# Moving a block of TensorE's program: even quads' P.V behind the loop's end, quad 1's keys directly behind quad 0's

## The chip, the cores and the metric

The kernel runs on one core of a Trainium2 chip. The metric is the device time of one execution in microseconds (us). Before the change it is 192.4 us, the median of three runs (191.73 to 192.55).

## What is computed

One decode step: attention of a single query over a cache of 4096 positions, 32 heads of 128, mixed by a gate with a small MLP. Cut from the reference:

```python
q = (x @ wq).reshape(B, Sq, Hq, Dh)                 # x: 1 x 512, 32 heads of 128
scores = einsum("bhqd,bhkd->bhqk", q, k) * (Dh ** -0.5)
p = softmax(scores)                                  # over 4096 positions
o = einsum("bhqk,bhkd->bhqd", p, v)
a = o.reshape(B, Sq, Hq * Dh) @ wo
h = relu(x @ w1 + b1); b = (h * h) @ w2 + b2
g = sigmoid((x * gate_w).sum(-1))
out = g * a + (1 - g) * b
```

Everything is bf16. Keys and values together are 67 MB of the 78 MB that are read; each is used once.

## The kernel before

**Tiling.** The 32 heads are handled as eight quads of four heads. A quad's keys are one tile of 128 partitions (32 per head) by 128 blocks of 128 numbers, loaded by one DMA of 4 MB; its values likewise. The four slots of `KV` hold two key tiles and two value tiles, so a quad's keys take the slot of the quad two before.

**A quad's work.** Of 128 key blocks, VectorE takes 48: a multiply and a sum over each of four parts of 12 blocks (`ttr`, L679 and L683). TensorE takes the other 80, in ten groups of eight: it transposes a group (`transposes`, L456), ScalarE copies the result to SBUF (`evac`, L351), and TensorE multiplies it with the query (`scores`, L463). `keys(a, behind)` issues the ten groups with the scores two groups behind the transposes; `a` is the parity of the quad. Then ScalarE copies the scores together (L357), VectorE takes the maximum per partition into `mp` (`smax`, L688), TensorE turns it into a row (`max_rows`, L484), VectorE reduces it (`gmax`, L692), TensorE spreads it again (`max_cols`, L488), ScalarE takes the exponentials (L368), and TensorE forms the denominators and P.V (`pv`, L493 and L497).

**The order of loads.** SyncE issues all large loads through one queue in a fixed order: wq, K0, K1, V0, w1, K2, wo's first quarter, K3, V1, K4, V2, K5, V3 and so on. A key tile is issued when its slot's last quad has been through VectorE's four parts (`s_sd`) and TensorE's ten groups of transposes (`s_t`); a value tile from V2 on when the P.V two before is done; wo's first quarter when the last of the query's eight projections is done (`s_qps`), which sits in `keys(1)` of the first turn. A load that waits holds all loads behind it.

**TensorE's program.** It is a loop written by hand with basic blocks, a register `turn_no`, branches and jumps; a turn handles an even and an odd quad. The blocks stand in the program in the order in which the code opens them: loop, h1, m1, m2, out, rows, first, k0, c1, v0, k1, r0, next, mlp, end. A branch whose target stands next falls through to it. In turn 0 the way is loop, first, k0 (`keys(0)`), r0 (`max_rows(0)`, `keys(1)`, `max_cols(0)`), next. From turn 1 on c1 (`max_cols(1)`) and v0 (`pv(0)`) come between k0 and r0; from turn 2 on also out and rows, blocks further up that are jumped to and come back by a jump to v0 and k1. Turn 4 runs only the odd quad's rest and the last even quad's P.V, with the MLP's first half (`mlp`) in between; turn 5 runs the last P.V and goes to `end`. In turn 0, then, k0 branches to r0 past c1, v0 and k1, 273 instructions; from turn 1 on c1 follows k0 in line and r0 follows k1 in line.

TensorE's whole program is 1748 instructions. `keys(1)`, with what stands between r0 and next, is 370 of them.

Of the kernel before, what the change touches and what calls it, by code (L numbers as in the profile page):

```python
# [5 lines left out]
def bass_gated_mix__gqa_block_cached__dense_activation_squared_relu__decode_kernel(  # L6
# [17 lines left out]
    ALU = mybir.AluOpType  # L24
# [55 lines left out]
    with ctx:  # L80
# [323 lines left out]
        def _(eng):  # L404
# [5 lines left out]
            turn_no = eng.alloc_register("turn_no")  # L410
# [3 lines left out]
            def at(name):  # L414
                stretch.close()
                if name == "end":
                    nc.switch_bb("pe_end")
                else:
                    stretch.enter_context(nc.body(f"pe_{name}", valid_engines=[mybir.EngineType.PE]))

            def go(name):
                eng.br(f"pe_{name}")

            def branch(op, n, then, other):
                eng.br_cmp(turn_no, n, f"pe_{then}", f"pe_{other}", op)

            def part(name):

                go(name)
                at(name)  # L430

            def only(name, op, n):

                branch(op, n, name, name + "_in")
                at(name + "_in")
# [14 lines left out]
            def take(sm, n=1):  # L450
                eng.wait_ge(sm, n).then_inc(sm, -n)  # L451

            def transposes(a, g):
                for y in range(GB):
                    b = Y_BLOCKS[GB * g + y]
                    mm = eng.transpose(KP[(GQ * a + g) % NKP][:, y * 128:(y + 1) * 128], key(a, b), ident[:, :])  # L456
                mm.then_inc(s_t, 1)

            def scores(a, g):
                take(s_ev)  # L460
                for y in range(GB):
                    c = GB * g + y
                    mm = eng.matmul(pS[:, R * c:R * c + R], kT[:, (GQ * a + g) % NT, y * 128:(y + 1) * 128],  # L463
                                    qc2[:, a, :], start=True, stop=True)
                mm.then_inc(s_s2, 1)

            def keys(a, behind):
                take(s_kp)
                for g in range(GQ):
                    transposes(a, g)  # L470
                    if g >= 2:
                        if g == 2:
                            take(s_q2)
                        scores(a, g - 2)
                    if g in behind:
                        only(f"q{a}{g}", "IS_GE", 1)
                        behind[g]()
                        part(f"q{a}{g}")
                scores(a, GQ - 2)
                scores(a, GQ - 1)  # L480

            def max_rows(a):
                take(s_mp)
                eng.transpose(MT, mp[:, a:a + 1], identf[:, :]).then_inc(s_mt, 1)  # L484

            def max_cols(a):
                take(s_dg)
                eng.matmul(MB[:, a:a + 1], dg[:, a, :], onesf[0:1, 0:1],  # L488
                           start=True, stop=True).then_inc(s_mb, 1)
# [62 lines left out]
            extra = [{}, {8: zero}]  # L552
# [52 lines left out]

            part("k0")
            keys(0, extra[0])
            branch("IS_LT", 1, "r0", "c1")
            at("c1")
            max_cols(1)  # L610
            branch("IS_GE", 2, "out", "v0")
# [2 lines left out]
            branch("IS_GE", 2, "rows", "k1")  # L614
            at("k1")
            eng.wait_ge(s_e, 1)
            part("r0")
            max_rows(0)
            keys(1, extra[1])
            max_cols(0)  # L620
            part("next")
            eng.reg_alu(turn_no, turn_no, 1, op=ALU.add)
            go("loop")

            at("mlp")
            mlp_h()
# [157 lines left out]
```

## Time and profile before

| | |
|---|---|
| time, median of 3 runs | 192.4 us (191.73 to 192.55) |
| profiled execution, its own time | 192.3 us |
| its span, first to last instruction | 190.8 us |
| mean granted TensorE clock | 0.727 |
| TensorE busy (matmul) | 136.8 us, 72% |
| VectorE busy | 122.5 us, 64% |
| ScalarE busy | 115.6 us, 61% |
| read from HBM | 78.32 MB, 410 GB/s over the span |
| queue q1 (all loads) | 4296 packets, 96.7% of 16 engines' span |
| queue q8 (kind: instruction) | 7 packets, 0.11 MB |

How to read it: the profile is one execution, and times within it count from the span's start. The engines are PE (TensorE's matmuls), PEld (its weight loads), DVE (VectorE), ACT (ScalarE), POOL (GpSimd) and SP (SyncE, which only issues loads here; SPq in the timeline). A timeline row gives start, duration, engine, line, operation, output and inputs, how many were merged, and in brackets how long the engine had been idle and what ended that. "PEq L451" is TensorE's own sequencer, at the semaphore step of the helper `take`; it stands there whatever the semaphore waited for. The DMA lines are shares of the core's 16 DMA engines and rates in equal slices. Each load also leaves 16 semaphore increments in the trace, one from each DMA engine; the last of them is the landing that the kernel waits for. Packets have a queue, a start, a duration and a size.

### The profile page before, as it was taken

Reading aid. Unit: us, or ns where it says so; the run is one execution under the profiler, and the core shown is the slowest. Engines: PE = TensorE matmul, PEld = TensorE weight load, DVE = VectorE, ACT = ScalarE, POOL = GpSimd, SP = SyncE. Lnnn points to the kernel's source line nnn. Section 1 sums busy time; section 2 is a strip of 40 time slices with the busy share of each in tenths; the row PEclk is TensorE's granted clock in tenths of the full one; section 3 lists DMA queues with packets and bytes.
Section 4 is the critical chain, followed back from the end, with each engine's and each line's share of the span. In section 5 each row is a group of like instructions: output and inputs, shape, how many; then the busy total and the mean of one; then the engine's idle time right before and its main releaser. Section 6 shows DMA issues by size and latency. Waiting matters only on the chain. (4 is left out here: it accounts for less than half of the span.)

```text
span 190.8 us, 6235 instructions
## 1 busy us (share of the span) xinstructions
PE 136.8 (72%) x2688; PEld 119.8 (63%) x2688; DVE 122.5 (64%) x123; ACT 115.6 (61%) x242; POOL 6.0 (3%) x13
## 2 busy tenths in 40 slices
PE   0009397607874979988995999769786596899855
PEld 0003176405763968977984997659575595789844
DVE  1100099989924999999999399829990699701011
ACT  3004669813998998798597569829961398450000
POOL 4000000000250000000000000000000000000000
PEclk9999969955897596695588559657955579555555
DMA  6999999989989999999999999999999999989991
GB/s 217 441 440 440 440 436 433 440 378 467 434 338 380 433 433 433 434 433 440 433 440 434 433 433 440 426 419 440 397 448 433 440 433 433 434 374 421 421 388 45
DMA packets 4321, 78.47 MB, mean 411 GB/s; under 512 B 499, under 2 KB 853, under 8 KB 1110
## 3 DMA queue, kind: packets, MB, share of 16 engines
q1 hardware_dynamic: 4296, 78.32, 96.7%
q8 instruction: 7, 0.11, 0.2%
q14 instruction: 4, 0.03, 0.0%
q10 hardware_dynamic: 14, 0.01, 0.0%
HBM read 78.32 MB, written 0.00 MB: 410 GB/s over the span
## 5 line engine op out<-in xcount | busy, mean ns | idle before, releaser
L351 ACT ACTIVATE kT<-KP 128x1024 bf16<-128x1024 bf16 x80 | 75.1, 1048 | 27.2 <-PE KP L456 27.1
L679 DVE TENSOR_TENSOR w2a<-KV,qb 128x1536 f32<-128x1536 bf16 x32 | 56.0, 1751 | 15.8 <-DMA KV<-in_A_k_cache_dram 15.4
L456 PE MATMUL KP<-ident,KV 128*128 128x128 bf16 x640 | 59.1, 254 | 7.4 <-PEq L451 7.4
L683 DVE TENSOR_REDUCE S<-w2a 128x12 f32<-128x1536 f32 x32 | 56.1, 1753 | 1.1
L456 PEld LDWEIGHTS KP<-ident,KV 128*128 128x128 bf16 x640 | 48.1, 115 | 10.6 <-issue 9.6
L463 PE MATMUL pS<-qc,kT 128*128 128x4 bf16 x640 | 28.1, 165 | 12.8 <-PEq L451 10.6
L463 PEld LDWEIGHTS pS<-qc,kT 128*128 128x128 bf16 x640 | 24.5, 99 | 18.9 <-issue 17.4
L497 PEld LDWEIGHTS pO<-E,KV 128*128 128x128 bf16 x1024 | 29.5, 105 | 1.8 <-issue 1.8
L497 PE MATMUL pO<-E,KV 128*128 128x4 bf16 x1024 | 28.7, 166 | 1.7 <-PEq L451 1.7
L368 ACT ACTIVATE E<-S,nM 32x128 bf16<-32x128 f32 x32 | 18.5, 577 | 0.9
L441 PE MATMUL pQ<-W,xb 128*128 128x512 bf16 x20 | 7.4, 512 | 12.9 <-DMA W<-in_A_wq_dram 11.9
L334 ACT ACTIVATE qb<-pQ 32x128 bf16<-32x128 f32 x20 | 5.4, 268 | 13.9 <-PE pQ L441 13.6
L441 PEld LDWEIGHTS pQ<-W,xb 128*128 128x128 bf16 x20 | 2.0, 117 | 15.1 <-DMA W<-in_A_wq_dram 12.0
L357 ACT ACTIVATE S<-pS 32x80 f32<-32x80 f32 x32 | 7.3, 228 | 4.8 <-PE pS L463 4.2
L658 DVE TENSOR_SCALAR e<-ez 128x1 f32<-128x1 f32 x1 | 0.2, 153 | 13.6 <-ACT ez L383 13.6
L484 PE MATMUL pM<-identf,mp 128*1 128x128 f32 x8 | 3.0, 372 | 8.2 <-PEq L451 7.9
L368 ACT ACTIVATION_READ_ACCUMULATOR E<-S,nM 32x1 f32 x32 | 8.0, 251 | 0.0
L702 DVE RECIPROCAL rden<-pO 128x4 f32<-128x4 f32 x8 | 1.4, 174 | 10.2 <-PE pO L497 10.2
L688 DVE TENSOR_REDUCE mp<-S 128x1 f32<-128x128 f32 x8 | 2.3, 286 | 7.2 <-ACT S L357 6.6
L484 PEld LDWEIGHTS pM<-identf,mp 128*1 128x1 f32 x8 | 0.6, 81 | 8.4 <-issue 8.4
L493 PE MATMUL pO<-RS,onesf 128*128 128x4 f32 x16 | 4.3, 340 | 1.3 <-PEq L451 1.3
L493 PEld LDWEIGHTS pO<-RS,onesf 128*128 128x128 f32 x16 | 3.8, 298 | 1.6 <-issue 1.6
(74 smaller groups left out, 71.1 us busy)
## 6 DMA issues: line engine op xcount, KB each, us to landing
KV<-in_A_k_cache_dram SPq DMA_DIRECT2D x8, 4096.0 KB, 20.7
KV<-in_A_v_cache_dram SPq DMA_DIRECT2D x7, 4096.0 KB, 26.0
W<-in_A_wq_dram SPq DMA_DIRECT2D x1, 4096.0 KB, 13.6
W<-in_A_wo_dram SPq DMA_DIRECT2D x4, 1024.0 KB, 17.5
KV<-in_A_v_cache_dram SPq DMA_DIRECT2D x4, 1024.0 KB, 13.6
w_sb<-in_B_w_dram SPq DMA_DIRECT2D x1, 1376.0 KB, 24.3
w2a<-in_B_w_dram SPq DMA_DIRECT2D x2, 512.0 KB, 14.2
w2a<-in_B_w_dram SPq DMA_DIRECT2D x2, 128.0 KB, 19.2
```

The source lines that it names most:

```text
L334: eng.activation(qb[rows(r), c, :], QR[c][rows(r), r * 128:(r + 1) * 128], ACT.Copy)\
L351: eng.activation(kT[:, n % NT, :], KP[n % NKP][:, :], ACT.Copy).then_inc(s_ev, 1)
L357: eng.activation(S[rows(r), q % NS, 0:YQ], S2[rows(r), :, r], ACT.Copy).then_inc(s_cp, 1)
L368: eng.activation(E[rows(r), q % 2, :, r], S[rows(r), q % NS, :], ACT.Exp, bias=nM[rows(r), q:q + 1], scale=SCALE, accum_out=RS[rows(r), q ...
L441: mm = eng.matmul(QR[c], xb[:, t, :], wq_sb[:, t, c * 512:(c + 1) * 512], start=(t == 0), stop=(t == 3))
L456: mm = eng.transpose(KP[(GQ * a + g) % NKP][:, y * 128:(y + 1) * 128], key(a, b), ident[:, :])
L463: mm = eng.matmul(pS[:, R * c:R * c + R], kT[:, (GQ * a + g) % NT, y * 128:(y + 1) * 128], qc2[:, a, :], start=True, stop=True)
L484: eng.transpose(MT, mp[:, a:a + 1], identf[:, :]).then_inc(s_mt, 1)
L493: eng.matmul(DEN[a], onesf[:, :], RS[:, a, :], start=True, stop=True)
L497: mm = eng.matmul(O[a], KV[:, V_SLOT[a], b * 128:(b + 1) * 128], E[:, a, COLUMN[b], :], start=(b == 0), stop=(b == NB - 1))
L679: eng.tensor_tensor(prod, KV[:, K_SLOT[q], x:x + XB * 128].rearrange("p (b d) -> p b d", d=128), qb[:, q, :].unsqueeze(1).to_broadcast([12 ...
L683: eng.tensor_reduce(S[:, q % NS, c:c + XB], prod, AX.X, ALU.add).then_inc(s_sd, 1)
```

## The change

The blocks r0 (with `max_rows(0)`, `keys(1)`, `max_cols(0)`) and next now stand directly behind k0; c1, v0 and k1 stand behind next. The branch at k0's end is turned round: turn 0 falls through to r0, later turns jump to c1. k1, which fell through to r0, jumps back to it. One instruction is added, that jump; no work on any engine is added, removed or reordered in time by the program itself.

```diff
             part("k0")
             keys(0, extra[0])
-            branch("IS_LT", 1, "r0", "c1")
+            branch("IS_GE", 1, "c1", "r0")
+            at("r0")
+            max_rows(0)
+            keys(1, extra[1])
+            max_cols(0)
+            part("next")
+            eng.reg_alu(turn_no, turn_no, 1, op=ALU.add)
+            go("loop")
+
             at("c1")
             max_cols(1)
             branch("IS_GE", 2, "out", "v0")
...
             at("k1")
             eng.wait_ge(s_e, 1)
-            part("r0")
-            max_rows(0)
-            keys(1, extra[1])
-            max_cols(0)
-            part("next")
-            eng.reg_alu(turn_no, turn_no, 1, op=ALU.add)
-            go("loop")
+            go("r0")
```

## The prediction, made before the changed kernel ran

> **What bounds the kernel now.** I read the page's slices and queues first, then the timeline of TensorE and VectorE around the jump, then the DMA view by windows, then SyncE's timeline. From the page, sections 2 and 3:
>
> ```profile
> DMA  6999999989989999999999999999999999989991
> GB/s 217 441 440 440 440 436 433 440 378 467 434 338 380 433 433 433 434 433 440 433 440 434 433 433 440 426 419 440 397 448 433 440 433 433 434 374 421 421 388 45
> ...
> q1 hardware_dynamic: 4296, 78.32, 96.7%
> q8 instruction: 7, 0.11, 0.2%
> ```
>
> The 16 DMA engines are busy in nearly every slice: 78.32 MB through one load queue fill 96.7% of the span, while the busiest compute engine (PE) has 72%. So loads set the end, and a stall on TensorE counts only if it leaves the load queue empty or lies behind the last load. Queue q8 is TensorE's own program arriving: seven packets of 16,384 bytes by the packet records (0.11 MB).
>
> The jump that the change takes out is visible in turn 0. From the timeline of 37 to 46 us (start, duration, engine, line, idle before):
>
> ```profile
> 37.54 0.34 PE L463 MATMUL pS<-qc,kT 128*128 128x4 bf16 x8 [0.58 <-PEq L451]
> ...
> 38.93 0.29 DVE L688 TENSOR_REDUCE mp<-S 128x1 f32<-128x128 f32 x1 [0.54 <-ACT S L357]
> ...
> 44.15 0.37 PE L484 MATMUL pM<-identf,mp 128*1 128x128 f32 x1 [6.27 <-PEq L451]
> ```
>
> `max_rows(0)` (L484) needs `mp`, which VectorE finishes at 38.93 + 0.29 = 39.22; TensorE starts it only at 44.15. One turn later the same operation for quad 1 is prompt:
>
> ```profile
> 59.80 0.29 DVE L688 TENSOR_REDUCE mp<-S 128x1 f32<-128x128 f32 x1 [6.08 <-ACT S L357]
> ...
> 60.68 0.37 PE L484 MATMUL pM<-identf,mp 128*1 128x128 f32 x1 [1.62 <-PEq L451]
> ```
>
> There it starts 60.68 - 60.09 = 0.59 us after `mp`. So in turn 0 some 44.15 - 39.22 - 0.59 = 4.3 us are not the wait for `mp`. "PEq L451" only names the sequencer's semaphore step. What lies in the hole is a program fetch, in the DMA view of 37.5 to 44.2 us, and none lies in the view of 60 to 165 us:
>
> ```profile
> q1 hardware_dynamic: 172, 2.81, 98.0%
> q8 instruction: 1, 0.02, 1.0%
> ```
>
> ```profile
> q1 hardware_dynamic: 1760, 45.09, 99.9%
> q14 instruction: 2, 0.02, 0.0%
> ```
>
> By the packet records the one of the hole runs from 41.54 to 42.61 us. The taken branch from `k0`'s end to `r0` passes c1, v0 and k1, 273 instructions of TensorE's program, and waits for code. The fetches where the code runs in line (28.27, 47.19, 54.41 us) show no such hole: TensorE's longest idle time beside them is 0.58 us.
>
> SyncE's timeline tells what the hole delays:
>
> ```profile
> 38.42 0.33 SPq L235 DMA_DIRECT2D KV<-in_A_k_cache_dram  x1
> 51.41 0.33 SPq L256 DMA_DIRECT2D W<-in_A_wo_dram  x1
> 56.64 0.33 SPq L235 DMA_DIRECT2D KV<-in_A_k_cache_dram  x1
> 57.02 0.43 SPq L240 DMA_DIRECT2D KV<-in_A_v_cache_dram  x1
> ```
>
> K3 (56.64) waits for quad 1's 80 transposes, V1 stands behind it in SyncE's order. In the DMA view of 36 to 84 us the slices are 1.2 us, about one 32 KB packet (counted at its start):
>
> ```profile
> GB/s 437 437 437 437 316 367 440 447 464 423 437 444 437 437 437 355 362 198 519 437 382 437 437 437 437 437 437 410 410 437 437 437 437 410 437 335 437 437 437 437
> ```
>
> A full slice has 437; the 18th (56.4 to 57.6 us) has 198: there the load queue ran dry.
>
> **The change part by part.**
>
> Turn 0, removed: the far jump, 4.3 us of TensorE. `max_rows(0)` comes at about 39.22 + 0.59 = 39.8, and `keys(1)`, which ScalarE's evacuations pace and which needs K1 (landed at 33.87), starts and ends some 4.3 us earlier. wo's first load goes from 51.41 to about 47, behind K2 as before. Quad 1's last transposes end at 56.57 - 4.3 = 52.3. What is late next for K3 is VectorE, whose four pairs for quad 1 end at 51.97 + 1.75 = 53.72 and were never held by TensorE. So K3 goes at about 53.75 instead of 56.64, with V1 behind it: 2.9 us earlier.
>
> What that is worth is the dry time alone. From the packets' starts and durations, the engines' idle time between 52 and 64 us is 0.61 us as a mean of 16; before it, from 12 us on, and after it up to 185 us, it is 0.03 us in all. With K3 at 53.75 there are still 1.5 MB queued (bytes issued less bytes moved), 3.4 us at the 437 GB/s of the full slices, so the hole closes wholly. It was not equal on all engines: the 16 landings of wo's first load run from 57.07 to 59.07, eleven of them up to 57.80 and five from 58.85, and those five never paused. The eleven lost up to 1.6 us each. A load is there when its last engine is. K3's last landing was 69.20; V1's, 4 MB later, 78.88, so 4 MB take 9.68 on the slowest engine. Without the hole K3's slowest engine is one of the five late ones, at 59.07 + 9.68 = 68.75: 0.45 us earlier. The bounds are 0 (the late engines set the last landing) and 1.6 (the engine with the longest pause sets it). At the end the last part of V7 lands from 181.63 to 183.54, with one engine 0.53 behind the others; a fetch at 171.84 lies shortly before. I take **0.5 us**, nearest to the K3 row and between 0.45 and the mean of 0.61.
>
> From there to the end: after 62 us TensorE waits for K loads (idle 1.79 at 127.92 and 3.65 at 149.84, right behind the landings of K6 and K7), and the tail from the last part of V7 (183.54) to 190.8 is the same code. So all of it moves up with the loads, by 0.5.
>
> Turns 1 to 3, added: a taken branch from `k0`'s end to `c1`, and one from `k1` back to `r0`; one instruction more in the program (`go("r0")`). What jumps cost when the code is there: loop's end back to its start, then h1's branches, three lines above with 0.59 us from `mp` to the matmul; from `max_cols(0)` to the next turn's DEN matmuls the idle time is 0.17 to 0.43 us (87.99, 121.92, 161.61). So at most 0.4 each, 0.8 a turn, 2.4 us in all on TensorE, below by 0. Cover: K4 to K7 are issued with 3.7, 8.4, 12.4 and 16.0 us of loads still queued (74.61, 89.72, 104.84, 123.16), so no issue is late enough to be felt; without that cover it would cost up to 2.4 us. I price it at nothing. If c1's code had to come once in turn 1, that is 4.3 us against the 8.4 queued at K5: nothing either.
>
> Turn 4 and the end: m1 to c1, mlp to v0, rows to next are taken jumps in both orders. Nothing.
>
> Sum: the profiled execution took 192.3 us (span 190.8, 1.5 around it). 192.3 - 0.5 = 191.8. The median of the three runs is 192.4, 0.1 above, so I forecast **191.9 us**. A measurement of this kernel can tell about 0.5%, 0.96 us, from no change; the gain is under that.
>
> [...] The row first: no q8 packet between 60 and 165 us, though the loop's three back jumps and its skips over pv(1), mlp, `out` and `rows` lie there. [...]
>
> **The rivals.**
> 1. *The late engines set the end, nothing gained.* For it: five engines had no pause at 57 us, and more fetches fall on the engines later. Against it: K3's last landing moved by 0.45 in the sum above. It gives 192.4. Chance 0.17. It is also what comes if the hole doesn't close, since TensorE's stall was hidden but for 0.6 us.
> 2. *Slower: the new jumps fetch again.* Place: k0 to c1 and k1 to r0, in turns 1 to 3; price 4.3 us each, from the hole. It decides where the delay passes the queued loads or meets the tail. In turn 3 the two would bring `max_rows(0)` from 145.81 to 154.4, so `keys(1)` to 154.6 instead of 149.84, 4.8 late; TensorE then has no pause over 0.7 us that could take it up until P.V of quad 7 (178.77, then 183.6). That needs 0.42 + 3.55 and ends at 187.5 instead of 184.73: 2.8 later, less 0.5, so 194.7. For it: one such jump did pay. Against it: no fetch in 105 us of looping. Chance 0.06.
> 3. *More is gained.* If the engine that paused longest (1.6 us) also ends last, 192.4 - 1.6 = 190.8. For it: the slowest K3 landing was one of the eleven. Against it: the five then come last. Chance 0.10.
>
> The forecast itself (191.5 to 192.3) has 0.67. The range that holds 8 in 10 reaches from 191.1, halfway into the third rival, to 192.7, the first with the spread of the runs (191.73 to 192.55). Chances: faster by over 0.5% 0.15 (0.10 of the third rival and 0.05 of spread below the forecast's edge), slower 0.07 (the second and 0.01 of spread), within 0.78.
>
> **What will show it.** Right: L484's first matmul at about 39.8 with under 1 us idle; K3 issued near 53.8; no slice near 198 GB/s around 57 us; seven q8 packets; K2 to K7 landing about half a us earlier. Wrong: a hole of 4 us at L488 or L484 in turns 1 to 3 with a q8 packet in it (second rival); a fetch hole in `keys(1)` of turn 0; or an unchanged dry slice at 57 us.

## The result and the profile after

The changed kernel takes 191.06 us (median of 7 runs, 190.81 to 191.22) against 192.4 (7 runs, 191.73 to 192.57). The ratio is 0.9938, with a 95% interval of 0.9921 to 0.9955: 1.34 us, or 0.6%, faster. The forecast had the direction and 0.5 us; the measured median lies 0.04 below the low end of its range. A time faster by over 0.5% had been given a chance of 0.15, one within 0.5% of before 0.78. The profiled execution took 190.93 us with a span of 189.6.

The timeline of the changed kernel from 37 to 46 us shows the hole gone. The scores of quad 0 end at 38.6, VectorE finishes `mp` at 39.66 + 0.29 = 39.95, and `max_rows(0)` starts at 40.09, so that its idle time is the wait for `mp`:

```profile
38.25 0.35 PE L463 MATMUL pS<-qc,kT 128*128 128x4 bf16 x8 [0.57 <-PEq L451]
...
39.66 0.29 DVE L690 TENSOR_REDUCE mp<-S 128x1 f32<-128x128 f32 x1 [1.27 <-ACT S L357]
...
40.09 0.37 PE L484 MATMUL pM<-identf,mp 128*1 128x128 f32 x1 [1.49 <-PEq L451]
```

SyncE's timeline has wo's first quarter at 47.36 instead of 51.41 and K3 at 54.76 instead of 56.64:

```profile
47.36 0.33 SPq L256 DMA_DIRECT2D W<-in_A_wo_dram  x1
54.76 0.33 SPq L235 DMA_DIRECT2D KV<-in_A_k_cache_dram  x1
55.13 0.43 SPq L240 DMA_DIRECT2D KV<-in_A_v_cache_dram  x1
```

And in the DMA view of 36 to 84 us the 18th slice, which had 198 GB/s, has 519 (the two before it, 355 and 369, were as low in before):

```profile
GB/s 437 437 437 437 312 385 436 447 462 437 437 437 437 423 437 355 369 519 505 437 437 437 437 437 437 410 437 437 437 437 423 437 410 444 382 437 437 437 437 410
```

The new far jumps cost TensorE nothing that can be seen. From the end of `keys(0)` over c1, v0 and back to r0 in turn 1:

```profile
67.88 0.34 PE L463 MATMUL pS<-qc,kT 128*128 128x4 bf16 x8 [0.58 <-PEq L451]
68.29 0.55 PE L488 MATMUL pM<-onesf,dg 1*128 1x1 f32 x2
68.77 0.59 PE L493 MATMUL pO<-RS,onesf 128*128 128x4 f32 x2
69.22 3.55 PE L497 MATMUL pO<-E,KV 128*128 128x4 bf16 x128
72.66 0.37 PE L484 MATMUL pM<-identf,mp 128*1 128x128 f32 x1
```

The last matmul of each block and the first of the next follow without an idle time in brackets (the longest gap is 68.29 - 68.22 = 0.07 us), although the way holds a jump over some 370 instructions and one back over more. The page counts seven program fetches again. By the landing records K3's last engine comes at 68.81 (before: 69.20), K7's at 148.99 (149.65), the last part of V7 at 182.32 (183.54): 0.39, then 0.66, then 1.22 us earlier.

### The profile page after: what moved, and what is told of

The parts are those of the page before. It is cut to its first block, busy times and chain, and to the rows that moved or that the text cites. A ratio compares the mean times of both kernels' runs of the same rounds, so it can differ in the third digit from the quotient of the medians.

```text
span 189.6 us, 6235 instructions
## 1 busy us (share of the span) xinstructions
PE 138.7 (73%) x2688; PEld 120.8 (64%) x2688; DVE 123.0 (65%) x123; ACT 115.9 (61%) x242; POOL 6.0 (3%) x13
## 5 line engine op out<-in xcount | busy, mean ns | idle before, releaser
L456 PE MATMUL KP<-ident,KV 128*128 128x128 bf16 x640 | 60.0, 256 | 9.2 <-PEq L451 9.1
L456 PEld LDWEIGHTS KP<-ident,KV 128*128 128x128 bf16 x640 | 48.9, 117 | 12.6 <-issue 11.7
L441 PE MATMUL KP<-W,xb 128*128 128x512 bf16 x12 | 4.9, 591 | 0.0
```

Of the source, the lines that this page charges most:

```text
L441: mm = eng.matmul(QR[c], xb[:, t, :], wq_sb[:, t, c * 512:(c + 1) * 512], start=(t == 0), stop=(t == 3))
```

## The experiments

**The kernel before again, twice.** No edit.

> The kernel before, unchanged, once more: its seven runs fall in two groups, near 191.75 and near 192.5. Theory (the load queue's dry slice, plus the DMA engine that a program fetch happens to fall on): the groups differ in the landing of the last part of V7, which was at 183.54 in the profiled run of 192.3; a run near 191.75 has it some 0.6 earlier, with the fetch of about 172 us on an engine that is not the slowest, and the dry slice near 57 us is there in both groups. Rival (TensorE's later work makes the time): the landings agree within 0.2 and TensorE's rows after the last landing differ. Median 192.2 +- 0.4 either way.

192.33 us over 12 runs, 191.44 to 192.68; ratio to other runs of before 0.9987 (0.9965 to 1.0008). Its profile (192.43) has the hole (max_rows(0) at 44.49) and K3's issue at 56.94; the last part of V7 lands at 183.82. The runs spread more than in two clean groups, and no execution near 191.4 was profiled, so the part on two groups stays untested.

> One more look at the kernel before. Theory: after the dry slice the first 32 KB packets take 1.4 to 2.2 us instead of 1.21, K3's median landing is 68.5 to 68.9 although wo's was 57.4 (the changed kernel: 67.2); time 191.4 to 192.7. Rival (the first slow packets were chance): the packets after the slice take 1.21.

192.56 us, one execution. The hole is shorter here (`max_rows(0)` at 42.89) and K3 goes out at 55.43, only 0.67 later than in the changed kernel. The slow packets are there, 29 of over 1.3 us between 50 and 90 us, up to 2.15. But K3's median landing is 67.96, not 68.5 to 68.9, and the dry time only 0.15 us; the last engine is 0.7 behind the next at K3 and 1.7 at V1. So the same time comes about with a small pause, 0.15 us of idle time and 0.75 of slow packets on the mean engine: here a queue that was almost dry cost as well.

**V1 ahead of K3, in the order of before.** TensorE keeps its hole; the queue gets 4 MB more.

```diff
-             "K0 K1 V0 K2 K3 V1 K4 V2 ..."
+             "K0 K1 V0 K2 V1 K3 K4 V2 ..."
```

> The order of before, with V1 issued ahead of K3: TensorE keeps its hole of 4.3 us at the far jump, but the load queue has 4 MB more in it at 57 us. Theory (the dry slice is what the hole costs): the slice near 57 us is full, K4 and later land 0.4 to 0.7 earlier than in before, and the time falls by 0.4 to 1.3, to 191.0 to 191.9, though max_rows(0) still starts near 44. Rival (TensorE's own lead, lost in turn 0, is what the end feels): still 192.4.

191.95 us over 12 runs, ratio 0.997 (0.9942 to 0.9998). In its profile (190.99 us, its median being 1 us higher) TensorE's hole is as long as ever, and the slice near 57 us is full. First the timeline's row, then the DMA view of 36 to 84 us:

```profile
44.05 0.37 PE L484 MATMUL pM<-identf,mp 128*1 128x128 f32 x1 [6.70 <-PEq L451]
```

```profile
GB/s 437 437 437 437 307 358 440 465 464 423 437 444 437 437 437 355 348 519 512 437 437 437 437 437 437 437 437 437 437 437 437 437 437 410 355 328 389 437 410 382
```

So an execution with the whole hole, but with a full queue at 57 us, can be 1.3 us shorter than the profiled one of before. The dip to 328 further right (the 36th slice, 78 to 79.2 us) is the queue's next thin place: K4, still issued late, at about 74.5. That may be why the median is only half way, just above the expected 191.9; but the profiled execution is one of the shorter ones, and no longer one was profiled, so it is not shown. The next run asks whether the order of loads itself costs.

**The same exchange in the changed order.**

> The changed order with V1 issued ahead of K3. With the order of before this exchange gave 191.95 in two groups (190.8 to 191.7 and 192.2 to 193.2) and left two engines dry for 0.5 us at 76.7, where K4 was issued late. Theory: TensorE's lead brings K4's issue forward to about 71, nothing runs dry, and the time is that of the changed kernel, 191.0 to 191.4. Rival (V1 ahead of K3 itself costs, or the groups come from the fetches alone): two groups again, median 191.6 to 192.3.

191.16 us over 9 runs (190.81 to 191.77), ratio 0.9946 (0.9927 to 0.9966). With TensorE's lead there, V1 ahead of K3 costs nothing that these runs can tell; the order of loads alone is not what kept the exchange at half way.

**TensorE held without a jump.** The changed order, with a wait that makes `max_rows(0)` late.

```diff
             at("r0")
+            eng.wait_ge(s_pd, NP + 2)
             max_rows(0)
```

> The changed order, with TensorE held in front of max_rows(0) by a wait for VectorE's second product of quad 1 (about 44.5 us), so that it loses in turn 0 what it lost at the jump, with no jump and no fetch waited for. Theory: K3 goes out near 57 again, the dry slice is back, 191.7 to 192.6. Rival (the jump or its fetch itself costs the time, not TensorE's late keys): as the changed kernel, 191.1.

192.97 us over 12 runs, ratio to before 1.0013 (0.9996 to 1.003). `max_rows(0)` starts at 45.43, 0.9 later than meant, K3 goes out at 57.93, and the dry time is 1.6 us. In the DMA view of 36 to 84 us four slices are thin:

```profile
GB/s 437 437 437 437 302 394 440 447 464 437 437 423 444 437 437 178 259 314 191 464 382 437 437 437 437 437 437 410 437 437 437 437 410 437 437 437 423 362 437 410
```

It is above the expected 192.6, with a pause longer than that of before. No jump is taken at this place, no fetch lies in the wait, and the whole gain is gone: it is TensorE's lateness at K3's release that costs, whatever causes it.

**Only K3 held.** TensorE runs early, SyncE issues K3 late.

```diff
+                if ORDER[n] == ("K", 3):
+                    eng.wait_ge(s_mt, 2)
                 load_kv(n)
```

> The changed order, with K3's load held until max_rows(1) is done (about 57.0 us, 0.4 after its issue in before); TensorE is not held. Theory: the dry slice is back and somewhat longer than in before, K3 lands last at 69.2 to 69.7, 191.7 to 192.8. Rival (TensorE's lead of 4 us is what is gained): 191.1 to 191.3.

192.32 us over 12 runs, ratio 0.9981 (0.9963 to 1.0). K3 goes out at 56.48 and the dry time is 0.65 us. The profiled execution is the slowest of the twelve, 193.31; in it K3's last engine lands at 71.39, not at 69.2 to 69.7, 2.5 us after the last but one, so its landings stand for a bad case. TensorE's `max_rows(0)` is prompt in the first row, at 39.56 (the lines are two further down in this kernel), and the load is late in the second:

```profile
39.56 0.37 PE L486 MATMUL pM<-identf,mp 128*1 128x128 f32 x1 [1.49 <-PEq L453]
```

```profile
56.48 0.33 SPq L235 DMA_DIRECT2D KV<-in_A_k_cache_dram  x1
```

With the exchange above, this tells where the gain lies. TensorE's lead without the earlier load is worth 0.17 us at the median, not clear of nothing; a full queue without TensorE's lead is worth 0.54 us at the median and 1.3 in the profiled execution.

**The changed kernel again.** No edit.

> The changed kernel once more, beside new runs of before. Theory (no dry slice; the engines that a program fetch fell on stay 1.3 us late while the other nine or so have slack that takes later fetches up): median 191.0 to 191.4; K3 lands on the median engine near 67.2 and last near 68.8; a run in which the fetch of 171 us falls on a late engine would be 192.2, so a few such runs may appear. Rival (the 7 runs so far were a lucky chip): 192.0 or more, no different from before.

190.87 us over 6 runs (190.77 to 191.0), ratio 0.9932 (0.9909 to 0.9955). The median is 0.13 below the expected range, and no run near 192.2 appeared.

**Code that is not there.** The changed order with instructions that never run between next and c1; in the built program the 1024 waits are 512 instructions.

```diff
-            go("loop")
+            branch("IS_GE", 99, "pad", "loop")
+            at("pad")
+            for n in range(1024):
+                eng.wait_ge(s_cst, 1)
+            go("c1")
```

> The changed order with 512 instructions that never run set between next and c1, so that in turn 1 the jump behind keys(0) goes to code that TensorE hasn't fetched. This is the place of the second rival of the prediction, made to happen once. Theory (TensorE's stalls count only against the loads still queued): a hole of 3 to 6 us in turn 1 before max_cols(1) or pv(0), with a q8 packet in it, K5 issued that much later (about 90 to 92) with some 5 us of loads still queued, no dry slice, and the time within 0.6 of the changed kernel. Rival (every stall of TensorE reaches the end): 4 us more, 195. If the loop no longer fits, a q8 packet comes in every turn and the time is 193 or more.

219.7 us, ratio 1.1435 (1.1396 to 1.1473), neither within 0.6 of the changed kernel nor the rival's 195: the program is fetched again and again, 23 times in all. The waits view of TensorE and the queues on the page:

```profile
PE pM L488 <- PEq L451: 22.9, 4, 7.5
...
PE pO L497 <- issue: 8.2, 3, 4.4
...
PE KP L505 <- issue: 4.5, 1, 4.5
```

```profile
q1 hardware_dynamic: 4296, 78.32, 84.8%
q8 instruction: 23, 0.38, 0.7%
```

The loop, from its start to k1's end, is 1955 instructions instead of 1443. There are 23 fetches instead of 7, and 11 of them lie between 60 and 165 us, where the changed kernel has one. `max_cols(1)`, the first matmul after the jump, is 22.9 us late in four turns, 7.5 at worst. The first turn bore out that cover, the loads still queued, decides: in turn 1 TensorE lost 7.5 + 4.4 us, K5 was issued at 93.76 instead of 86.37, still with 4.2 us of loads queued, and the engines' idle time from 64 to 100 us is 0.03. From turn 2 on the cover was used up: 2.0 us idle from 100 to 133, 10 us from 156 to 185, and then TensorE itself was behind.

**Visiting code ahead of time.** TensorE, idle until wq has landed, jumps to a block `warm` and back; in the order of before it stands directly ahead of r0, in the changed order directly ahead of end.

```diff
             mm.then_inc(s_xc, 1)
+            go("warm")
+            at("first2")
             eng.wait_ge(s_wq, 16)
...
+            at("warm")
+            eng.wait_ge(s_cst, 1)
+            go("first2")
```

> The order of before, but TensorE visits a one-instruction block directly ahead of r0 while it waits for wq (idle from about 2.5 to 14 us), so that r0's code is fetched then. The far jump at the end of quad 0's keys stays. Theory (the hole of turn 0 is the wait for code that is not there, and its price is the load queue's dry slice): a q8 packet more or earlier before 14 us, none in the hole, max_rows(0) at 39.8 to 40.3, K3 issued at 54 to 55, nothing dry, 190.8 to 191.5 as the changed kernel. Rival (a far taken branch costs 4 us wherever its target is, or the visit is forgotten by then): 192.0 to 192.7.

192.74 us over 12 runs, ratio 1.0011 (0.9995 to 1.0027). Two fetches more, at 6.45 and 12.33 us, and still one in the hole, at 40.43; `max_rows(0)` starts at 43.07. The DMA view of 37 to 43.1 us shows it:

```profile
q1 hardware_dynamic: 123, 2.32, 89.1%
q8 instruction: 1, 0.02, 1.0%
```

K3 goes out at 55.57. A fetch lay in the hole in spite of the visit, as the rival had it, so this run could not separate the code's absence from the branch.

> The changed order, with the same kind of visit to the code in front of the block end, so that the last code is fetched before 14 us and not at 171 us. Theory (in the changed kernel nine or so DMA engines have over 1 us of slack, so the fetch of 171 us falls mostly beside the path): 190.7 to 191.2, no difference from the changed kernel beyond 0.2. Rival (each program fetch delays the last landing by its 1.0 us): 189.7 to 190.2. If the visit pushes code out that is needed next, TensorE has a new hole before 25 us and the time is 192 or more.

190.93 us (190.9 to 191.07), ratio 0.9926 (0.9913 to 0.9939). The fetch near 171 us came all the same, at 171.52, so this visit did not spare the later fetch either, and the question about that fetch stays unanswered. What the run does show: nine fetches instead of seven, and no change in the time.

## Why the prediction was right in its direction and short in its size

**The bound was read rightly.** In the eleven profiles other than the padded kernel's, the time less the last landing of V7 is 8.6 to 8.8 us, whatever the order: loads set the end, and behind them is the same tail.

**The hole and its removal.** Expected at 39.8, `max_rows(0)` came at 40.09. Quad 1's last transposes, expected to end at 52.3, ended at 52.52, and VectorE was the last that K3 waited for, as forecast:

```profile
52.98 1.75 DVE L685 TENSOR_REDUCE S<-w2a 128x12 f32<-128x1536 f32 x1
```

That sum ends at 54.73 instead of 53.72: VectorE began quad 1 at 39.86 instead of 39.14, and one of its multiplies took 2.04 us instead of 1.76. So K3 came at 54.76, 1.0 us late but with 2.9 us of loads still queued. That the hole is a wait for code is supported: a fetch lies in it in each of the five profiles with the jump (41.54, 41.89, 40.29 and 41.47 us in before, its two repeats and the exchange, 40.43 with the visit), and `max_rows(0)` starts 1.5 to 1.7 us after that fetch ends, in all five, though the ends lie between 41.36 and 42.98. In the changed kernel no fetch lies between 37.5 and 44.2 us, and in the padded kernel, with its 23 fetches, the jump past the padding cost up to 7.5 us. A direct proof, the same jump with the code there, failed, since a fetch lay in the hole in spite of the visit (40.43).

**New jumps at nothing.** Right: in turns 1 to 3 no idle time stands before c1's first matmul (68.29, 99.50, 138.49) or before r0's (72.66, 106.46, 145.43), and there are seven fetches.

**The step that failed: "What that is worth is the dry time alone", with 0.5 us taken from K3's slowest engine.** That engine did what was worked out: 68.75 was expected and 68.81 came, 0.39 earlier. But by the end it was 1.22. The records of packets and landings tell what the sum had left out. Each row is one profiled execution; "idle" and "slow" are means of the 16 engines between 50 and 90 us, slow being the time of the 32 KB packets beyond 1.212 us each; "mean" and "last" are the mean and the last of the 16 landings of the last part of V7.

| kernel | time | idle | slow | mean engine | last engine | last less mean |
|---|---|---|---|---|---|---|
| before | 192.30 | 0.65 | 0.69 | 182.19 | 183.54 | 1.35 |
| before, again | 192.43 | 0.78 | 0.70 | 182.41 | 183.82 | 1.41 |
| before, a third time | 192.56 | 0.15 | 0.75 | 181.72 | 183.95 | 2.23 |
| before, with the visit | 193.13 | 0.28 | 0.71 | 182.07 | 184.40 | 2.33 |
| before, V1 ahead of K3 | 190.99 | 0.07 | 0.55 | 181.45 | 182.37 | 0.92 |
| only K3 held | 193.31 | 0.65 | 0.81 | 182.29 | 184.70 | 2.41 |
| TensorE held | 193.37 | 1.61 | 0.84 | 183.49 | 184.76 | 1.27 |
| changed | 190.93 | 0.00 | 0.28 | 181.18 | 182.32 | 1.14 |
| changed, again | 190.99 | 0.00 | 0.30 | 181.14 | 182.28 | 1.14 |
| changed, V1 ahead of K3 | 191.16 | 0.00 | 0.24 | 181.32 | 182.54 | 1.22 |
| changed, with the visit | 190.93 | 0.00 | 0.27 | 181.30 | 182.32 | 1.02 |

First, the dry queue cost its restart as well. Between 57 and 60 us of before, 15 packets of 32 KB took from 1.38 to 2.12 us where the same packets take 1.21; in the changed kernel, none did. That is 0.69 - 0.28 = 0.41 us on the mean engine, beside the 0.65 of idle time: 1.06 instead of the 0.61 that the prediction saw. The mean engine of before ends 1.01 later than that of the changed kernel, and in the other rows, too, idle and slow time tell within 0.2 us how much later it ends.

Second, the slowest engine at K3 is not the slowest at the end. The prediction let the five late engines, on which fetches had fallen, set the last landing, and counted the loss of the other eleven as slack. In before that slack is gone: at K3 the last engine is only 0.60 behind the median one, in the changed kernel 1.63. From there the changed kernel's lead at the last engine grew in each profile of before: from 0.39 at K3 to 0.66 at K7 and 1.22 at the end of V7, in the two repeats from 0.37 to 1.15 and 1.50, and from 0.82 to 1.78 and 1.63. In the first of them the last step comes late: 0.66 at the load that lands at 173.12, 1.20 at the next, shortly after the fetch of 171.84.

So of the 1.22 us, 1.01 lie on the mean engine, which the packets account for, and the other 0.21 in how far the last engine is behind it. This second part is no constant, and the mean alone doesn't give the end. The exchange in the order of before has a mean 0.27 later than the changed kernel and a last landing only 0.05 later; the visit in the changed order has two fetches more, a mean 0.12 later, and the same last landing; the third profile of before has the smallest mean loss of the three and the latest end. That later delays, such as fetches, fall beside the last engine in the changed kernel and on it in before is a reading of these records; no run moved a single fetch from one engine to another. Why the first packets after a pause are slow is open.

**The rivals.** "Nothing gained" was refuted by the interval, as was "more is gained" in its mechanism: no engine's 1.6 us alone set the end, though the size was nearest to it. The second rival, refetching, did not happen: one q8 packet lies between 60 and 165 us of the changed kernel, at 72.85, and there is no hole beside it (24 transposes run through from 72.82 to 75.58). Where it was made to happen, in a longer loop, its price was far too low, 194.7 against 219.7: the jumps cost up to 7.5 us each, not 4.3, P.V stalled again inside (4.4), and `max_cols(1)` was late in four turns. Of the fetches of before, the one at the far jump lies in a hole; those of code in line at 28.27, 47.19 and 54.41 us left none, the longest idle time beside them being 0.58 us. The loop of 1443 instructions went through 60 to 165 us with one fetch, the one of 1955 had 11 there. Why a fetch lay in the hole of before in spite of the visit is open.

## What to carry to other kernels

Where one load queue is full from start to end, look for the one slice in which it is not, find which wait let it run dry, and weigh a stall elsewhere only by that slice. Price such a slice by what the mean engine loses, its idle time plus the slow packets after it (here 0.65 and 0.41 us), and not by the landing of the slowest engine at that moment, which understated the loss at the end in all three profiles of before. The last engine's distance from the mean comes on top, and here it varied from 0.92 to 2.41 us between executions. Code on a first pass is best laid out in the order in which it runs: here a jump over 273 instructions cost TensorE 4.3 us in turn 0, and the fetches of code in line left it no idle time over 0.58. And the size of a loop is worth a look: with 1443 instructions it had one fetch from 60 to 165 us, with 1955 it had 11, and the time was 219.7 us.

## What the runs showed of the hardware that was not expected

- After a pause of the load queue, or when it was nearly dry, 15 or 16 packets of 32 KB took 1.3 to 2.2 us instead of 1.21, between 57 and 60 us of the three profiles of before. They came even where K3 was issued with 2.1 us of loads still queued (the third profile), and not with 2.9 (the changed kernel). The first packets of the whole kernel do the same: 15 to 18 of them were over 1.3 us before 12 us in each profile.
- A program fetch of 16,384 bytes took 0.93 to 1.1 us in before, and the fetches seem to come to one DMA engine after the other: the landings of K0, K1 and V0 in before have one, two and three engines some 1.3 us behind the rest, after one, two and three fetches.
- The far jump of turn 0, with a fetch in its hole (41.54), cost TensorE 4.3 us in before, and the jump past the padding up to 7.5 us in the padded kernel, with the load queue full. Where a block directly ahead of r0 had been visited by a jump there and back, with two fetches at 6.45 and 12.33 us, a fetch still lay in the hole at r0's first use, at 40.43.
